# A seven-product second layer over pairs of blocks

## The chip, the cores and the metric

One core of a Trainium2 chip runs the whole program. The metric is the device time of one execution in microseconds (us). Every kernel is run several times beside runs of the kernel before, on the same chip. A run is called slow when it is over 1.5% longer than the fastest of the same kernel, and comparisons use fast runs only. A ratio is the mean time of one kernel's fast runs over the mean of the other's fast runs of the same rounds, so it is not quite the ratio of the medians that are quoted.

The engines are named as in the profile: PE (matrix products), PEld (its weight loads), DVE (vector), ACT (scalar functions), POOL and SP (here they mostly issue DMAs). A q behind a name (SPq, POOLq) is the part of that engine that issues DMAs and waits. The profile gives DMA times as shares of 16 DMA engines. "Chain" is the work that ended last, followed back step by step to what released it.

## The reference

A gated recurrence over time, followed by a feed-forward layer with two branches and a maximum:

```python
# x, f_logit: (4, 6144, 256); w1, w2: (256, 1024); w_out: (1024, 256)
sig = 1 / (1 + exp(-f_logit));  f = lower_bound + (1 - lower_bound) * sig
h[t] = f[t] * h[t-1] + (1 - f[t]) * x[t]          # along time, per channel
g = maximum(h @ w1, h @ w2)                        # 24576 tokens
out = g @ w_out
```

Both kernels use max(a, b) = a + relu(b - a). With `wd` for the scaled w2 - w1 and `w13` for the scaled w1 @ w_out, the "first layer" is relu(y @ wd), and the "second layer" adds y @ w13 to relu(...) @ w_out.

## The kernel before: the parts that matter

The recurrence runs along time, and the program takes it with channels on partitions and tokens on the free axis (88 scans of 128x512 elements, 1.27 us each). Chunks of 1024 tokens therefore take a detour: a POOL DMA casts fp32 to bf16 from DRAM into a DRAM scratch ("cast"), and an SP DMA transposes the scratch into SBUF ("transpose"). There are two scratches for each of f_logit and x, used in turn, so the cast of chunk c+2 may start only when the transpose of chunk c has read its scratch. 22 of the 26 chunks go that way.

```python
# cast: one unbroken run of 1024 rows, written as 128 rows of 8 tokens
nc.gpsimd.dma_start(
    out=scr[0:nt, :].rearrange("(p i) d -> p (i d)", p=P),
    in_=src.rearrange("(p i) d -> p (i d)", p=P))
...
# transpose, issued later from SP
nc.sync.dma_start_transpose(out=dst[:, :, 0:nt], in_=held[c, s][0:nt, :])
...
# first layer: per block of 512 tokens and 128 hidden features
for kc in range(KC):
    nc.tensor.matmul(dT[:, 0:nb], lhsT=wd[:, kc, fc*P:(fc+1)*P], rhs=y[:, kc, 0:nb], ...)
nc.scalar.activation(out=rt[:, 0:nb], in_=dT[:, 0:nb], func=AF.Relu)
...
# second layer: 4 token tiles x 10 matmuls of 256 columns per block
left  = y[:, s, i:nb:ns] if s < KC else rts[j, s - KC][:, i:nb:ns]
right = w13[:, s, :]     if s < KC else wob[:, s - KC, :]
nc.tensor.matmul(ps[:, r, :], lhsT=left, rhs=right, ...)
```

## Time and profile before

| | before |
|---|---|
| time, median of 3 runs | 400.92 us |
| span of the profiled run | 428.3 us |
| PE busy in it | 392.8 us (92%) |
| chain of waits in it | PE 46%, DMA 34%, SP queue 15% |

The lines below are from the page of the kernel before: the span, the engine line (busy us, share of the span, number of instructions), two DMA queues (packets, MB, share of the 16 engines' span), the shares of the chain that ended last, two groups of instructions (busy us, mean ns, then idle time before them and who ended it), and two kinds of DMA issue (count, KB, median us from issue to landing).

```profile
span 428.3 us, 6970 instructions
PE 392.8 (92%) x2744; PEld 296.8 (69%) x2792; DVE 248.7 (58%) x359; ACT 268.5 (63%) x447; POOL 26.4 (6%) x58
...
q1 hardware_dynamic: 100512, 51.13, 66.7%
q0 software_dynamic: 2544, 25.17, 36.1%
...
PE 46%; DMA 34%; SPq 15%; ACT 3%; DVE 1%; issue 1%; ACTq 0%
...
L389 ACT ACTIVATE rt<-dT 128x512 bf16<-128x512 f32 x384 | 219.2, 598 | 104.1 <-PE dT L381 100.0
L381 PE MATMUL dT<-y,wd 128*128 128x512 bf16 x720 | 219.5, 384 | 21.3 <-ACT rt L389 19.5
...
scr_0_90<-in_f_logit_dram POOLq DMA_DIRECT2D x11, 512.0 KB, 7.5
scr_0_92<-in_x_dram POOLq DMA_DIRECT2D x11, 512.0 KB, 12.4
```

The casts are queue q0; the transposes are most of q1. A cast lands 7.5 to 13.6 us after its issue.

The next lines are from the timeline of PE, same kernel and run, in two short stretches (start us, us, engine, line, operation, output and inputs, shape, count): a row of transposes on PE near the start, and a dense stretch of the loop.

```profile
21.10 0.61 PE L180 MATMUL tT<-ident,fn 128*128 128x128 bf16 x8
21.55 0.61 PE L180 MATMUL tT<-ident,xn 128*128 128x128 bf16 x8
...
161.85 0.59 PE L381 MATMUL dT<-y,wd 128*128 128x512 bf16 x2
162.28 0.38 PE L410 MATMUL psO<-w_109,y 128*128 128x256 bf16 x2
162.50 0.49 PE L410 MATMUL psO<-wob,rt 128*128 128x256 bf16 x3
162.83 0.59 PE L381 MATMUL dT<-y,wd 128*128 128x512 bf16 x2
```

The feature blocks start 0.98 us apart. Two of them, with the 10 second-layer matmuls that go with them, take 1.953 us (a longer stretch of the same timeline gives the third digit) and hold 4608 columns, which is 2.36 columns per ns without a gap. That gives about 15.6 us for a pair of blocks. The eight 128-column matmuls fit in 0.61 us though one lasts 0.219 us, so they start (0.61 - 0.219) / 7 = 56 ns apart. In the same trace the next matmul starts 216, 109 and 56 ns after one of 512, 256 and 128 columns: from these three figures I estimate 0.417 ns per column (2.4 columns per ns) and 2.4 ns more for each matmul. For 512 columns that is the 215.7 ns of the prediction's sum.

### The profile page before, as it was taken

Reading aid. Unit: us, or ns where it says so; the run is one execution under the profiler, and the core shown is the slowest. Engines: PE = TensorE matmul, PEld = TensorE weight load, DVE = VectorE, ACT = ScalarE, POOL = GpSimd, SP = SyncE. Lnnn points to the kernel's source line nnn. Section 1 sums busy time; section 2 is a strip of 40 time slices with the busy share of each in tenths; the row PEclk is TensorE's granted clock in tenths of the full one; section 3 lists DMA queues with packets and bytes.
Section 4 is the critical chain, followed back from the end, with each engine's and each line's share of the span. In section 5 each row is a group of like instructions: output and inputs, shape, how many; then the busy total and the mean of one; then the engine's idle time right before and its main releaser. Section 6 shows DMA issues by size and latency. Waiting matters only on the chain.

```text
span 428.3 us, 6970 instructions
## 1 busy us (share of the span) xinstructions
PE 392.8 (92%) x2744; PEld 296.8 (69%) x2792; DVE 248.7 (58%) x359; ACT 268.5 (63%) x447; POOL 26.4 (6%) x58
## 2 busy tenths in 40 slices
PE   3999979798789999998997899999998999999996
PEld 1677756576557777776775577767676777777775
DVE  5785637455357566564653557657547656567551
ACT  3656656557366676675673666756657676776762
POOL 1400000000000000000000000000000000000000
PEclk9999999999989999999999699999999999999999
DMA  7999999999999999999998999999999999998112
GB/s 245 222 220 198 123 157 141 137 169 252 81 240 226 119 239 233 112 248 168 183 237 75 218 158 186 250 145 170 219 131 231 226 216 164 268 157 179 79 69 100
DMA packets 103377, 77.01 MB, mean 180 GB/s; under 512 B 93552, under 2 KB 94064, under 8 KB 102640
## 3 DMA queue, kind: packets, MB, share of 16 engines
q1 hardware_dynamic: 100512, 51.13, 66.7%
q0 software_dynamic: 2544, 25.17, 36.1%
q8 instruction: 22, 0.36, 0.4%
q10 hardware_dynamic: 288, 0.26, 0.2%
q14 instruction: 11, 0.09, 0.1%
HBM read 53.48 MB, written 48.23 MB: 237 GB/s over the span
## 4 chain that ended last, share of the span: by engine, by line
PE 46%; DMA 34%; SPq 15%; ACT 3%; DVE 1%; issue 1%; ACTq 0%
PE psO L410 25%; DMA fT<-scr_0_90 20%; PE dT L381 19%; SPq L153 13%; DMA fT<-scr_1_91 12%; ACT u L190 2%; DMA w1n_110<-in_moe_w_dram 2%; SPq L433 1%; PE psO L352 1%; ACT rt L389 1%; PE tT L180 1%; PE psO L365 0%; SPq L121 0%; DVE osb L430 0%; DVE y L233 0%
## 5 line engine op out<-in xcount | busy, mean ns | idle before, releaser
L389 ACT ACTIVATE rt<-dT 128x512 bf16<-128x512 f32 x384 | 219.2, 598 | 104.1 <-PE dT L381 100.0
L381 PE MATMUL dT<-y,wd 128*128 128x512 bf16 x720 | 219.5, 384 | 21.3 <-ACT rt L389 19.5
L410 PE MATMUL psO<-wob,rt 128*128 128x256 bf16 x1536 | 230.7, 274 | 2.7 <-issue 0.4
L410 PEld LDWEIGHTS <-rt 128*128 128x128 bf16 x1536 | 170.7, 114 | 41.4 <-issue 1.1
L233 DVE TENSOR_TENSOR_SCAN y<-ff,y,v 128x512 bf16<-128x512 bf16 x88 | 107.9, 1268 | 0.1
L430 DVE COPY osb<-psO 128x512 f32<-128x512 f32 x94 | 64.7, 690 | 59.0 <-PE psO L410 58.9
L381 PEld LDWEIGHTS <-wd 128*128 128x128 bf16 x768 | 75.8, 99 | 33.2 <-issue 24.6
L209 DVE TENSOR_SCALAR ff<-u,nom 128x512 bf16<-128x512 bf16 x94 | 29.0, 351 | 105.0 <-ACT u L190 105.0
L410 PE MATMUL psO<-w_109,y 128*128 128x256 bf16 x384 | 74.0, 275 | 0.0
L410 PEld LDWEIGHTS <-y 128*128 128x128 bf16 x384 | 43.4, 113 | 42.6 <-issue 3.5
L190 ACT ACTIVATE u<-fT 128x1024 bf16<-128x1024 bf16 x44 | 46.4, 1054 | 35.5 <-DMA fT<-scr_1_91 18.2
L220 DVE TENSOR_TENSOR v<-u,xT 128x1024 bf16<-128x1024 bf16 x44 | 30.3, 688 | 3.8 <-DMA xT<-scr_0_92 1.8
L98 POOL DMA_DIRECT2D scr_0_90<-in_f_logit_dram x11 | 5.4, 493 | 149.7 <-DMA fT<-scr_0_90 149.7
L98 POOL DMA_DIRECT2D scr_1_91<-in_f_logit_dram x11 | 5.3, 486 | 148.8 <-DMA fT<-scr_1_91 148.1
L233 DVE TENSOR_TENSOR_SCAN y<-ff,v 128x512 bf16<-128x512 bf16 x6 | 7.0, 1208 | 0.0
L98 POOL DMA_DIRECT2D scr_0_92<-in_x_dram x11 | 5.4, 488 | 18.7 <-DMA xT<-scr_0_92 16.9
L98 POOL DMA_DIRECT2D scr_1_93<-in_x_dram x11 | 5.3, 486 | 15.7 <-DMA xT<-scr_1_93 14.9
L190 ACT ACTIVATE u<-tT 128x1024 bf16<-128x1024 bf16 x3 | 3.2, 1058 | 4.3 <-PE tT L180 4.3
L352 PE MATMUL psO<-ident_f,w1n_110 128*128 128x128 f32 x8 | 1.9, 422 | 3.4 <-DMA w1n_110<-in_moe_w_dram 3.4
L341 ACT ACTIVATE wd<-wdf,om 128x128 bf16<-128x128 f32 (+1 forms) x6 | 2.2, 428 | 4.3 <-DVE wdf L333 4.3
L352 PEld LDWEIGHTS psO<-ident_f,w1n_110 128*128 128x128 f32 x8 | 1.6, 221 | 3.7 <-issue 3.7
L220 DVE TENSOR_TENSOR v<-u,tT 128x1024 bf16<-128x1024 bf16 x3 | 3.6, 1216 | 0.0
(49 smaller groups left out, 45.1 us busy)
## 6 DMA issues: line engine op xcount, KB each, us to landing
out_dram<-osb SPq DMA_DIRECT2D x47, 512.0 KB, 4.8
scr_0_90<-in_f_logit_dram POOLq DMA_DIRECT2D x11, 512.0 KB, 7.5
scr_0_92<-in_x_dram POOLq DMA_DIRECT2D x11, 512.0 KB, 12.4
scr_1_91<-in_f_logit_dram POOLq DMA_DIRECT2D x11, 512.0 KB, 7.9
scr_1_93<-in_x_dram POOLq DMA_DIRECT2D x11, 512.0 KB, 13.6
fn<-in_f_logit_dram POOLq DMA_DIRECT2D x3, 256.0 KB, 7.9
xn<-in_x_dram POOLq DMA_DIRECT2D x3, 256.0 KB, 8.6
w2n_112<-in_moe_w_dram SPq DMA_DIRECT2D x1, 512.0 KB, 6.5
```

The lines of the kernel that those rows point to most:

```text
L98: nc.gpsimd.dma_start(out=scr[0:nt, :].rearrange("(p i) d -> p (i d)", p=P), in_=src.rearrange("(p i) d -> p (i d)", p=P),)
L153: nc.sync.dma_start_transpose(out=dst[:, :, 0:nt], in_=held[c, s][0:nt, :])
L180: nc.tensor.transpose(dst, src, ident[:])
L190: nc.scalar.activation(out=like(u[:, :, 0:nb], fT), in_=fT, func=AF.Sigmoid, scale=-1.0)
L209: nc.vector.tensor_scalar(out=ff[:, h, 0:nb], in0=u[:, h, 0:nb], scalar1=nom[:, h : h + 1], scalar2=1.0, op0=ALU.mult, op1=ALU.add,)
L220: nc.vector.tensor_tensor(out=like(v[:, :, 0:nb], xT), in0=like(u[:, :, 0:nb], xT), in1=xT, op=ALU.mult,)
L233: nc.vector.tensor_tensor_scan(out=y[:, h, 0:nb], data0=ff[:, h, 0:nb], data1=v[:, h, 0:nb], initial=init, op0=ALU.mult, op1=ALU.add,)
L352: nc.tensor.transpose(pt[:, kc, q, :], half(w1n, g)[:, kc, 2 * r + q], ident_f[:])
L381: nc.tensor.matmul(dT[:, 0:nb], lhsT=wd[:, kc, fc * P : (fc + 1) * P], rhs=y[:, kc, 0:nb], start=(kc == 0), stop=(kc == KC - 1),)
L389: nc.scalar.activation(out=rt[:, 0:nb], in_=dT[:, 0:nb], func=AF.Relu)
L410: nc.tensor.matmul(ps[:, r, :], lhsT=left, rhs=right, start=(s == 0 and (r == 0 or j == NBLK - 1)), stop=(s == n - 1 and (r == 1 or j == N ...
L430: nc.vector.tensor_copy(out=osb[:, 2 * g : 2 * g + 2, :], in_=ps[:])
```

## The change

The intent is to save PE time. The second layer of two blocks is taken as a 2 by 2 block product and done with seven products instead of eight: 20480 columns per pair become 18432. The price is four sums on DVE and some snapshots on ACT. Chunks are wanted one to two pairs earlier. The casts were rewritten too: they go over the 1024 rows in runs of 8 tokens, every second run first and then the others, and are issued once both transposes of the chunk two back have landed ("the hold" below). The diff, cut to its core:

```diff
     def by_xbar(c, s):
-        return c >= 4
+        return chunks[c][2] == CH
@@ casts
-                nc.gpsimd.dma_start(
-                    out=scr[0:nt, :].rearrange("(p i) d -> p (i d)", p=P),
-                    in_=src.rearrange("(p i) d -> p (i d)", p=P),
-                )
+    def pieces(t):
+        return t.rearrange("(p a i) d -> a p (i d)", a=2, i=8)
+...
+            nc.gpsimd.dma_start(
+                out=pieces(scratch[s][c % NSCR][:]), in_=pieces(src)
+            )
@@ transposes, and the hold on the next casts
+        for s in range(2):
+            dst = inpool.tile([P, KC, CH], BF16, name=("fT", "xT")[s])
+            nc.sync.dma_start_transpose(out=dst[:], in_=scratch[s][c % NSCR][:])
+            held[c, s] = dst
+        if c + NSCR < NCHUNK:
+            for s in range(2):
+                pool_waits(held[c, s][:, 0, 0:1])
+            for s in range(2):
+                fetch(c + NSCR, s)
@@ first layer: two feature blocks per Relu
+        if fc % 2:
+            nc.scalar.activation(
+                out=rts[j, k][:, g - 1 : g + 1, :].rearrange("p q (i m) -> p q i m", m=P),
+                in_=dT[:].rearrange("p q (m i) -> p q i m", m=P), func=AF.Relu)
@@ second layer of a pair: 7 products of 16 matmuls and 4 linear parts of 8, 128 columns each
+        product("X", part(0, 0), lambda k: wob[:, k, lo], True)
+        then(snapshot("X", 1))
+        product("B", part(0, 1), lambda k: wob[:, KH + k, lo], True)
+        linear("B", ja, lo, False)
+        then(leave("B", ja, lo, 1, False))
+        product("X", sub(2), lambda k: t2[:, k, :])
+        then(snapshot("X", 2))
+        ...
```

(Cut: pools and buffers, the start-up, the slot schedule that interleaves first layer, products, scans and sigmoids, and the sums of the weights.)

## The prediction

> **What bounds the kernel now.** 400.9 us without the profiler; the profiled span is 428.3 us. Engine table: PE 392.8 us (92%), ACT 63%, DVE 58%. In the timeline of an undisturbed stretch (160 to 182 us), two first-layer feature blocks (4 matmuls of 512 columns) and 10 second-layer matmuls of 256 columns repeat every 1.953 us: [...] 7.81 us per 512-token block. 48 such blocks are 375 us; with the start (first big matmul at 13.1 us, then weights and transposes), and the tail I sum to about 398 us. So unprofiled, the kernel is almost free of stalls, while the profiled run loses some 25 us to DMA: its chain of waits has 34% on the f transposes and 13% on their issue. The packet records show why: a transpose alone takes 2.3 us and a cast alone 3.2 us, but where they overlap, both take about 10 us.
>
> **What the change does, per pair of blocks in steady state (21 of 24 pairs).**
> - PE: second layer 80 matmuls of 256 columns becomes 7x16+4x8 = 144 of 128 columns; 20480 columns become 18432. The question is whether 128-column matmuls, each with its own weight load, keep up. In the trace the 16 transposes in a row (128 columns, own weights) start 56 ns apart, on both the PE and the weight-load rows. [...] So 32x215.7 + 144x56 = 14.95 us, against 15.63: 0.68 us per pair, 14 us in all, all of it on PE and so critical.
> - DVE gains four sums of 2048 bf16 elements (estimate 1.15 us each, from the product of 1024 at 0.69 us[...]) and three additions (0.65), loses four evictions (0.69). About 13.4 us of 14.95: 90%.
> - ACT: 16 Relu of 0.60 become 8 of 1.05; 2 sigmoids of 1.05 become 4 of 0.60; plus four PSUM copies of 0.6: 13.1 us, 88%.
> Walking through the slots, each sum, snapshot and scan ends over 1 us before PE needs it, so I expect neither engine to bind.
> - DMA moves the same bytes. Casts held until both transposes landed keep them off the x transpose; steady state should then fit in 14.95 us, barely.
> - New risk: chunks are wanted one to two pairs earlier. Gates of the first paired chunks sit in ACT's queue at about 34, 42 and 52 us, while the profile of before transposes them at 32-39, 44-62 and 67-82. ACT is in order, so Relu, then PE, stop: I estimate 4 to 6 us lost at the start.
>
> **Time.** 400.9 - 14.3 + 5 - 1.6 (start-up stalls that before already has) gives about 390 us. Range 383 to 400. Faster by over 2%: 0.62; within 2%: 0.34; slower: 0.04.
>
> **What would show it.** 128-column matmuls at 56 ns spacing in the timeline; pair period of 14.95 us in late windows; PE busy with few gaps after 100 us; the wait list showing ACT sigmoids waiting for f transposes before 80 us; casts and x transposes no longer overlapping; DVE near 90%, ACT near 88% in late windows.
>
> **What would make it wrong.** Weight loads from strided y slower than 56 ns; the strided PSUM read slowing Relu, so that ACT binds; DVE falling behind the sums; DMA not keeping 14.95 us per chunk, which would give back most of the gain; a start-up stall of 15 us or more rather than 5.

400.9 - 14.3 + 5 - 1.6 is 390.0 us. That ACT holds back its Relu behind a waiting sigmoid, and PE with it, shows later in the run with an outer dimension of 16: four sigmoids wait 5.66 us, the next Relu starts at 39.76 us, and PE waits 3.80 us for it.

## More of the kernel before

The profiled run was 28 us longer than the timed ones. It was a slow run, as a later profile showed. These lines are from that later profile's page (span, engines, chain by engine, and the casts):

```profile
span 399.1 us, 6970 instructions
...
PE 386.1 (97%) x2744; PEld 295.3 (74%) x2792; DVE 249.0 (62%) x359; ACT 269.5 (68%) x447; POOL 26.4 (7%) x58
...
PE 95%; DMA 2%; DVE 1%; issue 1%; SPq 1%
...
scr<-in_f_logit_dram POOLq DMA_DIRECT2D x22, 512.0 KB, 6.2
scr<-in_x_dram POOLq DMA_DIRECT2D x22, 512.0 KB, 8.0
```

And from its timeline of SP:

```profile
227.87 2.57 SPq L153 DMA_TRANSPOSE fT<-scr  x1
230.53 3.20 SPq L153 DMA_TRANSPOSE xT<-scr  x1
...
243.51 2.65 SPq L153 DMA_TRANSPOSE fT<-scr  x1
```

The chain is 95% PE, a cast lands after 6.2 to 8.0 us, and one chunk starts every 15.64 us. The kernel before is bound by PE.

## The result

The changed kernel took 719.49 us (median of 4 runs, 714.87 to 723.97), against 401.01 us for the kernel before. The ratio of the fast runs is 1.79 (95% interval 1.786 to 1.803). The prediction said 390 us and faster.

From the page of the changed kernel, in the same views as above: span, engines, queues, the chain by engine and by line, three groups, and the DMA issues.

```profile
span 718.4 us, 9570 instructions
PE 427.7 (60%) x4136; PEld 308.5 (43%) x4136; DVE 325.7 (45%) x383; ACT 290.1 (40%) x383; POOL 56.5 (8%) x98
...
q1 hardware_dynamic: 100512, 51.13, 93.9%
q0 software_dynamic: 46896, 25.33, 24.1%
...
DMA 91%; PE 6%; POOL 1%; SPq 1%; issue 0%; ACT 0%; DVE 0%; POOLq 0%; ACTq 0%
DMA xT<-scr 61%; DMA fT<-scr 19%; DMA scr<-in_f_logit_dram 11%; PE ps L603 3%; PE dT L425 2%; PE ps L472 1%; DMA r<-in_moe_w_dram 1%; SPq L151 0%; SPq L118 0%; POOL fT L106 0%; POOL xT L106 0%; POOL wob L629 0%; ACT sn L549 0%; SPq L618 0%; POOL waited L338 0%
...
L603 PE MATMUL ps<-t,S 128*128 128x128 bf16 x1008 | 96.7, 250 | 252.9 <-ACT sn L549 204.6
...
L274 ACT ACTIVATE u<-fT 128x512 bf16<-128x512 bf16 x88 | 55.0, 628 | 304.8 <-DMA fT<-scr 304.8
...
scr<-in_f_logit_dram POOLq DMA_DIRECT2D x22, 512.0 KB, 25.6
scr<-in_x_dram POOLq DMA_DIRECT2D x22, 512.0 KB, 26.2
```

Now DMA is 91% of the chain, and PE only 6%. The sigmoids on ACT (L274) wait 305 us for f transposes, and the products on PE (L603) wait 253 us, 205 of which ended with a snapshot on ACT. The bytes of q0 are the same, 25 MB, but its packets went from 2544 to 46896, and a cast lands after 26 us instead of 6 to 8 (the fast profile of before; 7 to 14 in the slow one).

The timeline of SP in one period of the changed kernel:

```profile
315.80 5.04 SPq L151 DMA_TRANSPOSE fT<-scr  x1
321.35 20.32 SPq L151 DMA_TRANSPOSE xT<-scr  x1
341.78 0.99 SPq L444 DMA_DIRECT2D out_dram<-osb  x2
344.69 4.96 SPq L151 DMA_TRANSPOSE fT<-scr  x1
```

And its timeline of POOL in the same period:

```profile
319.42 0.79 POOL L101 DMA_DIRECT2D scr<-in_f_logit_dram  x1
320.20 0.79 POOL L101 DMA_DIRECT2D scr<-in_x_dram  x1
```

One chunk takes 344.69 - 315.80 = 28.9 us where PE needs 15 (14.95 us in the later run with an outer dimension of 16). The casts are issued at 319.4 and 320.2 us, and the x transpose that starts just after them holds SP for 20.3 us. It took 3.2 us in the fast profile of before.

The trace also records each DMA packet. A count of these records by size:

```
                      packets of one cast    4-byte records per cast, above     casts' packets started
                                             the 816 of before in all           per us in mid-cast
before                16 of 32 KB              0                                -
changed              128 of  4 KB            896 = 14 x 64                     12, steady from 326 to 342 us
```

The packets' times show how many are under way at once. In the kernel before a cast by itself had 16 under way (median) and took 3.3 us, and no more than 16 packets of casts were under way at any time. In the changed kernel it is 2 for a cast by itself (the two that ran from 157.6 and 181.8 us took 23.4 and 24.3 us), and 4 (median) where both casts of a chunk run. The trace lists the cast as 16 runs of 32768 bytes, which is 16384 elements, in the kernel before, and as 2x64 runs of 4096 bytes, 2048 elements, in the changed one, with the 2 outermost in the diff. So for a cast by itself the packets under way are as many as the outer dimension listed, in both. The 4-byte records (called fillers below) fit that count: with k for the outer dimension, (16 - k) x 128 / k is 14 x 64 = 896 for 2 and 0 for 16. What they are for, the trace does not say.

### The profile page after: what moved, and what is told of

Its sections match the earlier page's. It is cut to its first block, busy times and chain, and to the rows that moved or that the text cites. A ratio compares the mean times of both kernels' runs of the same rounds, so it can differ in the third digit from the quotient of the medians.

```text
span 718.4 us, 9570 instructions
## 1 busy us (share of the span) xinstructions
PE 427.7 (60%) x4136; PEld 308.5 (43%) x4136; DVE 325.7 (45%) x383; ACT 290.1 (40%) x383; POOL 56.5 (8%) x98
## 3 DMA queue, kind: packets, MB, share of 16 engines
q0 software_dynamic: 46896, 25.33, 24.1%
## 4 chain that ended last, share of the span: by engine, by line
DMA 91%; PE 6%; POOL 1%; SPq 1%; issue 0%; ACT 0%; DVE 0%; POOLq 0%; ACTq 0%
DMA xT<-scr 61%; DMA fT<-scr 19%; DMA scr<-in_f_logit_dram 11%; PE ps L603 3%; PE dT L425 2%; PE ps L472 1%; DMA r<-in_moe_w_dram 1%; SPq L151 0%; SPq L118 0%; POOL fT L106 0%; POOL xT L106 0%; POOL wob L629 0%; ACT sn L549 0%; SPq L618 0%; POOL waited L338 0%
## 5 line engine op out<-in xcount | busy, mean ns | idle before, releaser
L603 PE MATMUL ps<-t,S 128*128 128x128 bf16 x1008 | 96.7, 250 | 252.9 <-ACT sn L549 204.6
L603 PEld LDWEIGHTS <-S 128*128 128x128 bf16 x1344 | 107.4, 112 | 302.4 <-issue 227.5
L433 ACT ACTIVATE r<-dT 128x1024 bf16<-128x1024 f32 x192 | 196.1, 1024 | 100.5 <-PE dT L425 99.4
L274 ACT ACTIVATE u<-fT 128x512 bf16<-128x512 bf16 x88 | 55.0, 628 | 304.8 <-DMA fT<-scr 304.8
L561 DVE TENSOR_TENSOR osb<-ps,sn 128x512 f32<-128x512 f32 x63 | 43.4, 689 | 249.1 <-PE ps L603 240.9
L603 PEld LDWEIGHTS <-r 128*128 128x128 bf16 x1008 | 66.9, 98 | 27.3
L603 PEld LDWEIGHTS <-y 128*128 128x128 bf16 x672 | 55.0, 120 | 21.8 <-issue 8.9
L603 PE MATMUL ps<-w,y 128*128 128x128 bf16 x504 | 55.8, 240 | 0.0
L494 DVE TENSOR_TENSOR S<-r 128x2048 bf16<-128x2048 bf16 x42 | 51.1, 1217 | 5.5 <-ACT r L433 5.5
L494 DVE TENSOR_TENSOR S<-r,S 128x2048 bf16<-128x2048 bf16 x42 | 50.8, 1210 | 0.9 <-ACT r L433 0.9
L603 PE MATMUL ps<-wob,r 128*128 128x128 bf16 x672 | 51.2, 219 | 0.0
L603 PE MATMUL ps<-wob,S 128*128 128x128 bf16 x336 | 31.2, 228 | 0.0
L603 PE MATMUL ps<-t,r 128*128 128x128 bf16 x336 | 29.0, 219 | 0.0
```

Of the source, the lines that this page charges most:

```text
L274: nc.scalar.activation(out=mids[p + NBLK, "u"][:, h, cols], in_=held[c, 0][:, h, cols], func=AF.Sigmoid, scale=-1.0,)
L433: nc.scalar.activation(out=rts[j, k][:, g - 1 : g + 1, :].rearrange("p q (i m) -> p q i m", m=P), in_=dT[:].rearrange("p q (m i) -> p q i ...
L494: nc.vector.tensor_tensor(out=t[:], in0=a, in1=b, op=op)
L561: nc.vector.tensor_tensor(out=dst, in0=bank[b][:], in1=snap[name][:], op=ALU.add)
L603: nc.tensor.matmul(bank[b][:, i, :], lhsT=a, rhs=w, start=fresh, stop=after is not None, skip_group_check=True,)
```

## The experiments

Theory E: with an outer dimension of 2 only 2 packets of a cast are under way at once, casts take longer, and transposes beside them wait. Rivals: G, the hold chains casts and transposes; S, small packets or the row order are slow; P, the new second layer or its schedule is what costs the time.

All twelve runs gave correct results. The profile does not record which DMA engine carried a packet, so what the recorded expectations say of engines was the author's inference; it is cut, and the cut marked, as is a remark on what the other 4-byte records are.

### One unbroken run per cast, the rest as changed

```diff
-        return t.rearrange("(p a i) d -> a p (i d)", a=2, i=8)
+        return t.rearrange("(p i) d -> p (i d)", p=P)
```

> The changed kernel with one part undone: each cast is again one unbroken run of 1024 rows, as in the kernel before; the hold on casts and the seven products stay. Theory E [...]: casts land in under 10 us instead of 25, the period of a pair falls from 28.6 us to about 15, and the time to 385-400 us. Rival G (the hold strings casts and transposes into one chain): still over 600 us. Rival P (the second layer itself needs more): between, over 420 us with DMA waits gone.

Measured: 396.06 us (393.64 to 419.98, one of four slow), ratio 0.986 (0.980 to 0.991). 320 us are gone with this line, while the hold and the seven products stayed. In its profile, which is of the slow run, casts landed after 7.7 and 9.8 us (f and x) and the median period was 13.6 us, so those parts of the expectation held too. G and P fall as main causes.

### Outer dimension of 16, and of 4, with the same 8-token runs

```diff
-        return t.rearrange("(p a i) d -> a p (i d)", a=2, i=8)
+        return t.rearrange("(p a i) d -> a p (i d)", a=16, i=8)     # and a=4
```

> The changed kernel with the same 8-row runs and the same 4 KB descriptors, but an outer dimension of 16 instead of 2. Theory E: as fast as the unbroken run, 385-400 us, with descriptors still of 4096 bytes and no 4-byte fillers [...]. Rival S (small descriptors or the interleaved row order are what is slow): still over 600 us.

Measured: 392.10 us (fast runs 390.15, 391.53, 392.67; one slow at 400.03), ratio 0.976 (0.973 to 0.980), faster than the kernel before. Its casts still are 128 packets of 4 KB in interleaved order, so S falls. Its page has:

```profile
span 389.4 us, 9498 instructions
...
PE 370.6 (95%) x4064; PEld 278.1 (71%) x4136; DVE 321.6 (83%) x383; ACT 288.5 (74%) x383; POOL 42.8 (11%) x98
...
PE 88%; issue 1%; ACT 1%; DVE 0%
...
scr<-in_f_logit_dram POOLq DMA_DIRECT2D x22, 512.0 KB, 7.4
scr<-in_x_dram POOLq DMA_DIRECT2D x22, 512.0 KB, 10.0
```

And its timeline of SP:

```profile
229.03 2.62 SPq L151 DMA_TRANSPOSE fT<-scr  x1
231.75 9.23 SPq L151 DMA_TRANSPOSE xT<-scr  x1
...
243.98 7.81 SPq L151 DMA_TRANSPOSE fT<-scr  x1
```

The chain is PE again, casts land in 7 to 10 us, and a period is 14.95 us.

> The changed kernel with an outer dimension of 4. Theory E: [...] the two casts of a chunk take about 11 us rather than 21 (24 packets of 4 KB start per us rather than 12), the period about 17 to 18 us, the time 430-480 us; 768 rather than 896 fillers of 4 bytes per cast. Rivals G and S: no change, about 720 us.

Measured: 491.08 us (two fast runs 478.77 and 483.86, two slow to 514.29): far from 720 us, the fast runs around the upper end of the expected 430 to 480 us. The two casts of a chunk took 11.7 us (median, from the packet records), 24 packets started per us, and most periods were 17 to 19 us. The number of fillers was mis-stated: 384 per cast, not 768. It is what (16 - k) x 128 / k gives for k = 4, 12 times 32, as 14 times 64 was for k = 2.

### Without the hold, outer dimension of 2

```diff
-            for s in range(2):
-                pool_waits(held[c, s][:, 0, 0:1])
```

> The changed kernel with an outer dimension of 2 as it is, but without the hold: a cast is issued when its own scratch is free. Theory E: casts still take 21 us for a chunk, so still over 600 us, perhaps 5 to 10% off. Rival G: 385-420 us.

Measured: 1019.81 us, ratio 2.54. G predicted the opposite, so it is out. But I also had the sign of the side effect wrong: the hold saves 300 us. The timeline of SP of this run shows how:

```profile
391.45 21.95 SPq L151 DMA_TRANSPOSE xT<-scr  x1
413.49 1.01 SPq L442 DMA_DIRECT2D out_dram<-osb  x2
414.63 23.18 SPq L151 DMA_TRANSPOSE fT<-scr  x1
437.91 21.98 SPq L151 DMA_TRANSPOSE xT<-scr  x1
```

The timeline of POOL, with the idle time before each issue and who ended it:

```profile
406.64 0.79 POOL L101 DMA_DIRECT2D scr<-in_f_logit_dram  x1 [31.40 <-DMA fT<-scr]
420.85 0.79 POOL L101 DMA_DIRECT2D scr<-in_x_dram  x1 [13.42 <-DMA xT<-scr]
```

Here the two casts are issued 14 us apart and run one after the other. 6 packets start per us for most of the time, half as many as with the hold, and each cast stretches one transpose to 22 us, so a chunk takes 46.5 us. With the hold, both casts are issued in one go and 12 packets start per us: the pair is done in 22 us, and only one transpose is caught. So two casts side by side took no longer than one. The rates also speak against two rivals that I had not named, that the fillers or the making of so many records are what is slow: one cast by itself took 21 to 25 us here, and with the hold two casts, with twice the records, took 22 us together.

Why a transpose suffers at all: the trace shows 2048 packets of 256 bytes for one transpose. Their mean time was 106 ns in the changed kernel (182 ns here) against 27 ns with an outer dimension of 16, and the median is 18 to 25 ns in all three, so a minority waits long. Of the 2048 packets of an x transpose, 660 (median) took 300 to 700 ns in the changed kernel, about 184 with an outer dimension of 4 and 10 with 16; of an f transpose in the changed kernel, which meets 2 cast packets (median), none (median). One 4 KB cast packet took 322 ns (median), so the slow transpose packets took about as long as one or two of those. That they waited behind them is the author's reading; the trace does not show it.

### Outer dimension of 8, and the hold with an outer dimension of 16

> The changed kernel with an outer dimension of 8. [...] Theory E: [...] 5.5 to 7 us for the two casts, 128 fillers of 4 bytes per cast; about as fast as with 16, 390-405 us. [...]

Measured: 407.27 us, of which 402.81 and 404.87 in fast runs; ratio 1.007 (0.996 to 1.018). The two casts took 7.2 us, about 48 packets started per us, and there were 128 fillers per cast, as expected. The time lies at the upper end: 11 to 13 us slower than with an outer dimension of 16, against a run of another batch, which I did not take apart further. Its profile is of a slow run; in it four of the 22 pairs of casts took 12.8 to 18.4 us, and a transpose beside each took 12.3 to 17.3 us, where with an outer dimension of 16 no pair took over 11.4 us. That is a hint and no more.

In this batch five of the eight runs of the kernel before were slow.

> The changed kernel with an outer dimension of 16 and no hold on the casts. [...] the hold was worth 300 us, because it let the two casts run side by side. If that was all, without the hold 390-394 us, the same as with it. If the hold also keeps casts off the transposes to a purpose: 396-410 us, with the x transpose's data time up from 5 us towards 8 and the periods over 14.95 us.

Measured: 426.74 us (416.27 and 422.34 in fast runs), ratio 1.065 (1.061 to 1.070). So with an outer dimension of 16 too the hold is worth some 28 us for this kernel, as the fast means of 419.3 and 391.5 us show (two batches, on two chips), more than I allowed for. In its profile, a fast run, an f transpose moved its data in 8.4 us (median), an x transpose in 2.1 us, and most periods ran from 13 to 20 us; with the hold it was 3.2 us for f, 5.1 us for x, and most late periods were 14.95 us. So the x transpose went the other way than I expected: the hold moves the casts from the f transposes onto the x transposes. Without it f transposes are 42% of the chain, and ACT's sigmoids wait 30 us for them; with it they are not in the chain, and the sigmoids wait 5.7 us.

The series, with the period taken from the starts of successive f transposes:

```
outer dim   hold   4-byte fillers   casts' packets   both casts     period of    time
                   per cast         started per us   of a chunk     a chunk
   2        no     896 = 14 x 64     6               45.5 us        46.5 us      1019.8 us
   2        yes    896 = 14 x 64    12               22.0 us        28.6 us       719.5 us
   4        yes    384 = 12 x 32    24               11.7 us        18   us       491.1 us
   8        yes    128 =  8 x 16    48                7.2 us        14.95 us      407.3 us
  16        yes      0              48                6.3 us        14.95 us      392.1 us
```

(Medians over the chunks of each trace, the profiles of the first and the second-to-last line being of slow runs; for 8 and 16 the period is that of the late chunks, where PE sets the pace; "per us" is the usual count in mid-cast; times are medians of all runs.) With 2 of its 128 packets under way at once, a cast is 64 turns, and 22 us is 0.344 us per turn (an estimate; a packet took 322 ns, median, in the changed kernel). From that alone, 128/k turns give 22, 11 and 5.5 us for k of 2, 4 and 8, if the outer dimension sets the packets under way there as it did in the two kernels above. At 16, I estimate 5.5 us again, from 256 packets of both casts in 16 turns, if no more than the 16 of the kernel before are under way at once; the starts per us, 48 as at 8, fit that. Measured were 22.0, 11.7, 7.2 and 6.3 us.

### The same casts in the kernel before

```diff
-                    out=scr[0:nt, :].rearrange("(p i) d -> p (i d)", p=P),
-                    in_=src.rearrange("(p i) d -> p (i d)", p=P),
+                    out=scr[0:nt, :].rearrange("(p a i) d -> a p (i d)", a=2, i=8),
+                    in_=src.rearrange("(p a i) d -> a p (i d)", a=2, i=8),
```

> The kernel before with one thing changed: its casts get the outer dimension of 2. Theory E: the same DMA-bound period as the changed kernel without the hold, 45 to 48 us per chunk, so 980-1050 us, with a second layer that was never touched. Rival (the new schedule, which wants its chunks earlier, is what makes the casts matter): under 500 us.

Measured: 1032.80 us, ratio 2.577, period 46.5 us per chunk. From its page, span and chain by engine:

```profile
span 1034.0 us, 6970 instructions
...
DMA 51%; SPq 22%; PE 19%; DVE 5%; issue 2%; ACT 1%; POOL 0%; ACTq 0%
```

The outer dimension of 2 alone, in a kernel whose second layer and schedule were never touched, does the whole damage. P is out.

> The kernel before with its casts in 8-row runs under an outer dimension of 16. It is bound by PE at 15.63 us per chunk without the profiler, so casts that are no slower leave it there: 399-403 us. Set against the changed kernel with the same casts and no hold it gives the worth of the second layer alone: 10 to 14 us expected.

Measured: 400.75 us, ratio 1.000 (0.998 to 1.002), all four runs fast. As said before the run, PE binds, so casts that are no slower change nothing. The second half of that expectation, to read the second layer's worth from the pair without the hold, was of no use, because the changed kernel needs the hold and this one does not.

### The hold in the kernel before, and the start-up

> The kernel before with casts under an outer dimension of 16 and with the hold (a cast waits for both transposes of the chunk two back). It had periods of 15.6 us without the hold, so PE binds: 400-402 us with it too. Then the changed kernel [...] against this one differs in the schedule and the second layer alone, and its 9 us are theirs. If the hold costs the kernel before something: over 405 us.

Measured: 400.27 us, ratio 0.999 (0.997 to 1.000). The hold costs the kernel before nothing. With casts and hold alike, the changed kernel's fast mean of 391.5 us against 400.3 us is worth 8.8 us for the second layer and its schedule (two batches; the median of the kernel before was 401.10 us in one and 401.15 us in the other).

The steady period fell by 0.69 us (15.64 to 14.95), which over 21 pairs is 14.5 us, so 5.7 us are given back somewhere. The timeline of the version with an outer dimension of 16 shows most of it:

```profile
37.67 2.19 ACT L274 ACTIVATE u<-fT 128x512 bf16<-128x512 bf16 x4 [5.66 <-DMA fT<-scr]
...
40.82 2.72 PE L425 MATMUL dT<-y,wd 128*128 128x512 bf16 x6 [3.80 <-ACT r L433]
```

There is one PE gap of 3.80 us, behind sigmoids that waited 5.66 us for the first paired chunk's f transpose. The windows view of the same run (stretch, us, then busy time of PE, PEld, DVE, ACT and POOL, granted clock, DMA share, GB/s) shows the clock after it:

```profile
40.00:50.00 10.00, 9.13 (x51) 5.45 (x52) 5.18 (x9) 7.43 (x9) 1.20 (x3) 0.83 1.13 218
150.00:225.00 75.00, 74.16 (x866) 56.20 (x881) 66.76 (x76) 60.02 (x81) 9.61 (x21) 1.00 1.10 215
```

(The DMA share is the packets' time over that of 16 engines; at 1.13 and 1.10 here, packet records overlap.) The trace's clock record has half the clock from 40.12 to 43.53 us, which makes the mean of 0.83. PE was still idle until 40.82 us, so 2.71 us of work ran at half clock (its weight loads for 512-column matmuls start 0.42 to 0.43 us apart, where such matmuls started 0.216 us apart at full clock), a loss of some 1.4 us; with the gap that is 5.2 us. The rest I did not find. Half clock came 3.1 us into the gap; what brought it about is not shown.

I tried to take this gap away, by issuing the four sigmoids after the Relu of the next block, and then also queueing that chunk's f cast earlier:

```diff
             if fc < 3:
                 early[fc]()
-            if fc % 2:
-                pair_gate(PAIR0, fc // 2)
         early[3]()
         for fc in range(FC):
             first_layer(2, fc)
+            if fc in (3, 7):
+                pair_gate(PAIR0, fc // 4 * 2)
+                pair_gate(PAIR0, fc // 4 * 2 + 1)
```

> The changed kernel with the outer dimension of 16, and the four sigmoids of the first paired chunk issued after the Relu of block 2 instead of before. [...] the profile shows one wait of 5.66 us on ACT at 32 to 37.7 us for that chunk's f transpose, PE idle 3.8 us at 37 to 40.8 us, and the clock at half for 3.4 us after it (1.7 us): 5.5 us in all. Theory: this is the start-up loss of 4 to 6 us that the prediction named, and the move takes most of it away, at the cost of some waiting for ACT: 386 to 390 us, no PE idle over 1.5 us before 60 us. Rival (the next gap only moves there): 391-393 us, as with the order unchanged.

> As the run before it, and the f cast of the first paired chunk is queued before the loads of the third directly loaded chunk, so that its transpose can start some 2 us sooner. Expected 385 to 389 us, at most 1.5 us under the run before it; if those loads were needed at once, as much over it.

Measured: 400.77 us (389.66 to 403.24) and 397.08 us (390.03 to 397.75). Only one run of each counts as fast, at 389.66 and 390.03 us, beside 390.15 to 392.67 us for the version they start from. So no gain is shown: 389.66 us lies just inside the 386 to 390 us expected of the first move, but it is one run, 390.03 us misses the expectation of the second, and the medians are worse. Both profiles are of slow runs, and I build on one thing in them only as a hint: the early gap is gone (0.93 us is left), but a gap of 7.47 us, or 3.45 us, ends at 105 us, or 104 us. Whether the gap only moves, as the rival says, is not settled.

### The kernel before in its fast state

> The kernel before, once more, for a profile in its fast state; the profile at hand is of a run of about 430 us. If the 25 us of difference are DMA waits of casts in 32 KB packets beside transposes: a span of 399 us, periods of 15.6 us per chunk and f transposes moving in about 3 us where the slow run had 8.4.

Measured: 400.81 us, span 399.1 us, periods of 15.6 us, and a transpose's data moved in 2.4 us (f) and 2.5 us (x). The slow profile that the prediction worked from had an f transpose of 8.4 us; so its 28 us were a state of that run, not of the kernel. What brings that state about is not shown.

## Why the prediction was wrong, point by point

- **What bounds the kernel before**: right. In the fast state PE is 95% of the chain, and the period is 15.64 us.
- **128-column matmuls at 56 ns, 14.95 us per pair**: right. The version with an outer dimension of 16 has 14.95 us per pair, and its second-layer matmuls start 56 ns apart, as the PE transposes of the kernel before do.
- **DVE at 90% and ACT at 88%, neither binding**: right for DVE, and ACT was over-estimated. In the window from 150 to 225 us DVE is busy 66.8 of 75 us (89%) and ACT 60.0 (80%). The sums took 1.21 us, where 1.15 was estimated.
- **Start-up loss of 4 to 6 us**: right in size, 5.2 us in the version with an outer dimension of 16, though of the three waits that I had named only the first is there, with a loss of clock behind it.
- **"DMA moves the same bytes. [...] steady state should then fit in 14.95 us, barely."** This step failed. The bytes are the same (25.17 and 25.33 MB), but in the runs the time of casts followed their outer dimension: 22.0, 11.7, 7.2 and 6.3 us for both casts of a chunk with 2, 4, 8 and 16. I read the new access pattern as a matter of row order, gave it no cost at all, and left it out of what could go wrong except as "DMA not keeping 14.95 us". It was 22 us per pair of casts with 2, a transpose caught behind them, 28.6 us per chunk and 327 us in all. With the one number changed from 2 to 16, the kernel runs at 392.1 us, where the prediction said 390.
- **The hold keeps casts off the x transpose**: wrong. The next chunk's transposes are under way by then: with an outer dimension of 16, at 231.75 us, an x transpose holds SP for 9.23 us beside casts issued at 229.8 us. What the hold keeps free is the f transpose (3.2 us with it, 8.4 us without). Its worth is large all the same: 28 us in fast means with an outer dimension of 16, 300 us with 2.

What stays open: why the changed kernel needs the hold with an outer dimension of 16 while the kernel before does not (without the hold its transposes moved their data in 3.0 and 2.7 us, so the casts hardly slowed them there; it has 0.7 us more room per chunk, but that this is the reason was not tested), and why an outer dimension of 8 was 11 to 13 us slower than 16 though its casts took only 0.9 us more.

## What to carry to other kernels

When a DMA's access pattern is rewritten, look at its outermost dimension before its bytes: here an outer dimension of 2 made the two casts of a chunk take 22.0 us instead of the 6.3 us with 16, and it also dragged down the transposes (22 us instead of 2.4). The share of the casts' queue hides this, as it fell from 36% to 24%; the number of packets, the time to landing and the DMA's part in the chain of waits show it. If interleaving is wanted, a dimension of 16 outermost is what was best here: the version that does so has the lowest median, at 0.976 of the kernel before.
